# The end of the first phase of a long-convolution kernel: the last rows of the first two pairs are copied straight from result tiles, and the stores and the filter's work there are placed anew

## The chip, the cores and the metric

The kernel runs on one core of a Trainium2 chip. The metric is the time of one execution on the device in microseconds (us); the median of the runs is compared. Engines are named as in the profile: PE (TensorE), DVE (VectorE), ACT (ScalarE), POOL (GpSimd) and SP (SyncE, which here only issues DMAs). A DMA can be issued by SP, ACT or POOL; each of the three has its own queue, and the profile shows an issue by SP or ACT as an instruction of SPq or ACTq.

## The reference

```python
def _attn_ref(x, v, pos_emb, w1, w2):            # x, v: (4, 12800, 128)
    h_filt = (np.maximum(pos_emb @ w1, 0.0) @ w2) * np.exp(-0.01 * pos)[:, None]
    u = x * v
    Uf = np.fft.rfft(u, n=2 * S, axis=1)         # S = 12800
    Hf = np.fft.rfft(h_filt, n=2 * S, axis=0)
    y = np.fft.irfft(Uf * Hf[None], n=2 * S, axis=1)[:, :S]
    return x * y
...
def _moe_ref(x, w_val, conv_w, w_out):           # x is what _attn_ref returned
    gate = sigmoid(causal convolution of x over 5 steps, by channel)
    return (gate * (x @ w_val)) @ w_out
```

So the kernel multiplies x by v, convolves the product along the sequence with a filter as long as the sequence, multiplies by x again and passes the result through a small gated layer.

## The kernel before, in words

The sequence of 12800 is cut into two halves of 6400 (index j), and each half into 100 x 64 (indices n1 and n2). A transform over n1 and one over n2 take the place of the long transform. The kernel has three phases that follow one another, because each needs what the one before left in memory (the HBM).

**First phase** (`signal`, lines 357 to 406, and `filt`, 225 to 297). For each of the 64 values of n2, SP loads 100 rows of x and v (line 312), DVE multiplies them and forms sums and differences (`prep`: lines 323, 334, 335, 342), PE transforms over n1 (line 391, two halves c = 0 and 1 of four records each), ACT copies each half from PSUM into a result tile `st` (line 392), and the tile is stored to `a_u` in HBM (line 400). The tile has 2 x 1024 numbers on each of 100 partitions: the partition is the frequency k of the transform over n1, spread over the 128 partitions by the table `PARTS` (64 frequencies on the even partitions, 32 and 4 between them). The store is three DMAs: frequencies 0 to 63 by ACT, 64 to 95 by POOL, and 96 to 99 by POOL one n2 later (`flush`, line 415). For the last two n2 (62 and 63) the first of them is cut again: frequencies 0 to 3 by SP, 4 to 63 by ACT. An even n2 fills rows n2 and n2 + 1 of `a_u`, an odd one rows 63 + n2 and 64 + n2; so n2 62 fills rows 62 and 63, and n2 63 rows 126 and 127.

Between these, the filter's own transform is advanced step by step. A list `due` (lines 419 to 422) has three spans with a number of steps each; a step is run when the loop has reached its n2. The third span has 26 steps from n2 38.5 on, spread over 22 n2. One step of it has 8 matmuls of PE (16 records, line 292), four scaled copies and one PSUM copy of ACT (lines 279 and 295) and one product of DVE (line 280). The order on every engine is the order in which the program is written (`manual_schedule`).

**Second phase** (from line 462, its loop from 552). It goes over 50 pairs p of frequencies. Pair p takes frequencies 2p and 2p + 1 of all 128 rows of `a_u` (1 MB, `load_a`, line 201) and filter values (`filter_pair`); PE transforms over n2 into `z_ps` (`spectrum`, line 491, 8 records), DVE multiplies by the filter in four instructions (va, vb, vc, vd, line 497), POOL adds (lines 578 and 581), PE transforms back, and the results are stored. `spectrum` of a pair needs all of its 128 rows.

At the border the loads of pair 0 are cut into EARLY rows (0 to 55 and 64 to 119), loaded when n2 = 58 is reached, and LATE rows (56 to 63 and 120 to 127), loaded when the first phase is written out. Pair 1 is loaded behind them, with pairs 2 and 3 after it. On PE, `filter_pair(0)` and ten matmuls whose results nobody reads (lines 561 to 564) come between the last n2 and the first `spectrum`.

**Third phase** (from line 613). Rows of the result are loaded, transformed and gated; PE bounds it.

The loads of x and v go through a ring of nine tiles; a tile is loaded again when the n2 that read it are done (`release`, `fetch`). Two of the last results use tiles of that ring (`SPARE`): n2 61 one of the extra tiles, n2 63 the tile that pair 2 is loaded into afterwards.

Of the kernel before, what the change touches and what calls it, by code (L numbers as in the profile page):

```python
# [23 lines left out]
B, S, D, FO, KC = 4, 12800, 128, 64, 5  # L24
# [93 lines left out]
def tile_longconv_gate(  # L118
# [20 lines left out]
    nc = tc.nc  # L139
# [45 lines left out]
    BD = B * D  # L185
    NP = N1 // 2
    PG = KG // 2
    EARLY, LATE = (slice(0, 56), slice(64, 120)), (slice(56, 64), slice(120, 128))
    weights, loaded = {}, {}

    def load_w(p):
# [17 lines left out]
    with tc.tile_pool(name="p1", bufs=1) as p1, tc.tile_pool(name="ps1", bufs=1, space=PSUM) as ps1:  # L209
# [147 lines left out]
        def signal():  # L357
            fetch(4)
            load_pos(0)
            fetch()  # L360
            load_pos(HC)
            ready = [prep(0)]
            for n in range(N2):
                if n == 8:
                    nc.gpsimd.dma_start(out=dft, in_=t_dft)
                    nc.gpsimd.dma_start(out=tw, in_=t_tw)
                    nc.gpsimd.dma_start(out=inv, in_=t_inv)
                if n == 12:
                    for dst, src in ((wval, w_val), (wout, w_out), (cw, conv_w.rearrange("k d -> d k"))):
                        raw = p1.tile(list(dst.shape), mybir.dt.int64, name=f"raw{len(raws)}")  # L370
                        nc.gpsimd.dma_start(out=raw, in_=src)
                        raws.append((dst, raw))
                if n in (18, 22, 26):
                    _narrow(nc, p1, *raws[n // 4 - 4])
                if n == BACK + 2:
                    load_w(0)
                if n == N2 - 6:
                    for part in EARLY:
                        load_a(0, part)
                if n + 1 < N2:  # L380
                    ready.append(prep(n + 1))
                both = ready.pop(0)
                if n in SPARE:
                    st = next(t for i, t in ring if i == SPARE[n]).rearrange("p (c e) -> p c e", c=2)
                else:
                    st = p1.tile([128, 2, J * BD], F32, name="st", bufs=4)
                for c in range(2):
                    fp = ps1.tile([128, J, BD], F32, name="fp", bufs=2)
                    for j in range(J):
                        h = slice(j * 64, j * 64 + 64)  # L390
                        nc.tensor.matmul(out=fp[:, j], lhsT=fsd[h, c], rhs=both[c][h], start=True, stop=True)  # L391
                    nc.scalar.copy(out=st[:, c], in_=fp.rearrange("k j e -> k (j e)"))  # L392
                    yield
                src = st.rearrange("k c e -> k (c e)")
                row = n % 2 * N2 + n // 2 * 2
                dst = a_u[:, row:row + 2].rearrange("k c e -> k (c e)")
                for eng, (k0, k, step, p0) in zip((nc.scalar, nc.gpsimd), PARTS):
                    cuts = [0, 4, k] if k0 == 0 and n >= N2 - 2 else [0, k]
                    for a, b in zip(cuts, cuts[1:]):
                        (nc.sync if b == 4 else eng).dma_start(  # L400
                            out=dst[k0 + a:k0 + b], in_=src[p0 + step * a:p0 + step * (b - 1) + 1:step])
                if n % 2 == 1:
                    release()
                rest.append((dst, src))
                if len(rest) > 1 or n + 1 == N2:
                    flush()
# [10 lines left out]
        n_done = [False]  # L417

        due, t0 = [], 3
        for n, w in ((J * N2 // 4 + 2, 15.5), (FO // 2, 20), (N1 // 4 + 1, 22)):  # L420
            due += [t0 + w * i / n for i in range(n)]
            t0 += w
        sig, fil = signal(), filt()
# [38 lines left out]
    with tc.tile_pool(name="p2", bufs=1, reuse_waits="tile") as p2, \  # L462
# [89 lines left out]
        with tc.manual_schedule():  # L552
            for p in range(-1, NP + 2):
                now, nxt, old = 0 <= p < NP, p + 1 < NP, 0 <= p - 1 < NP
                if p < 0:
                    z_first = new_z()
                    for part in LATE:
                        load_a(0, part)
                    for part in EARLY + LATE:
                        load_a(1, part)  # L560
                    filt_p[0] = filter_pair(0)
                    for _ in range(10):
                        w_ps = ps2.tile([128, 2, BD], F32, name="c_ps", bufs=2)
                        nc.tensor.matmul(
                            out=w_ps[:, 0, 0:2 * D], lhsT=ident, rhs=dft.rearrange("p a k -> p (a k)"), start=True, stop=True)
                if (p + 3) % PG == 0 and p + 3 < NP:
                    load_w(p + 3)
                for q in range(2, AHEAD) if p < 0 else (p + AHEAD,):
                    if q < NP:
                        load_a(q, slice(0, 2 * N2))  # L570
                if now:
                    h = filt_p.pop(p)
                    z0, z1 = z_p.pop((p, 0)), z_p.pop((p, 1))
                    va = p2.tile([128, 2 * J, B, D], F32, name="va", bufs=3)
                    vb = p2.tile([128, 2 * J, B, D], F32, name="vb", bufs=2)
                    times(va, z0[:, 0], h[:, 0], 2 * J)
                    times(vb, z0[:, 1], h[:, 1], 2 * J)
                    (nc.gpsimd if nxt else nc.vector).tensor_tensor(va[:, 0:2], va[:, 0:2], vb[:, 0:2], op=ALU.add)  # L578
                    apart = p % 6 == 5
                    if not apart:  # L580
                        nc.gpsimd.tensor_tensor(va[:, 2:4], va[:, 2:4], vb[:, 2:4], op=ALU.add)  # L581
                if nxt:
                    z_p[p + 1, 0] = spectrum(p + 1, 0, z_first if p < 0 else None)
                if now:
                    vc = p2.tile([128, 2, B, D], F32, name="vc", bufs=2)
                    vd = p2.tile([128, 2, B, D], F32, name="vd", bufs=2)
                    times(vc, z1[:, 0], h[:, 0, 0:2], 2)
                    times(vd, z1[:, 1], h[:, 1, 0:2], 2)
                    v_p[p] = [va[:, 2:4]] + [vb[:, 2:4]] * apart + [vc, vd]
                if now and not nxt:  # L590
                    inverse(p, va[:, 0:2])
                if old:
                    inverse_half(p - 1, v_p.pop(p - 1))
                if p + 2 < NP:
                    filt_p[p + 2] = filter_pair(p + 2)
                if nxt:
                    z_p[p + 1, 1] = spectrum(p + 1, 1)
                if now and nxt:
                    inverse(p, va[:, 0:2])
                if 0 <= p - 2:  # L600
                    butterfly(p - 2)
                for s, c, i in early.get(p, ()):
                    load_part(s, c, i)
# [277 lines left out]
```

## Time and profile before

| | |
|---|---|
| median of 3 runs | 1068.43 us (1066.77 to 1068.98) |
| the profiled execution's own time | 1070.6 us |
| its span in the profile | 1068.8 us |
| mean granted clock of TensorE | 0.977 |
| busy share of the span | PE 92%, DVE 91%, ACT 58%, POOL 70% |
| DMA traffic | 330.16 MB, mean 309 GB/s |

Times in the trace count from the span's start; the profiled execution's own time is 1.8 us more than its span. The numbers in brackets behind an engine's row are the idle time ahead of the instruction and what ended it. The first phase ends near 314 us, the second near 676 us.

### The profile page before, as it was taken

To read this page: it belongs to the slowest core of one execution; us is meant where nothing else is said; L and a number is where in the kernel's file an instruction comes from. 1 tells how busy PE (TensorE), PEld (TensorE's weight loads), DVE (VectorE), ACT (ScalarE), POOL (GpSimd) and SP (SyncE) were. 2 spreads that over 40 slices of the span, in tenths; PEclk is the share of its full clock that TensorE was granted. 3 is DMA by queue.
4 is the path that set the end of the run, shared out by engine and by line. 5 is a ranking of instruction groups with operands and counts; after the bars stand their busy time and mean duration, and the time that the engine had idled before them with its cause. 6 is when DMAs were issued, how large, how long until landed. Compare 5 with 4: busy or idle time off the path is not lost. (4 is left out here: it accounts for less than half of the span.)

```text
span 1068.8 us, 21559 instructions
## 1 busy us (share of the span) xinstructions
PE 980.4 (92%) x8100; PEld 510.5 (48%) x8100; DVE 972.3 (91%) x1061; ACT 624.9 (58%) x1017; POOL 747.6 (70%) x465
## 2 busy tenths in 40 slices
PE   2768799989998999999999999679999999999996
PEld 0344466656644555455445545334444444444442
DVE  8868999599948999999989999279999999999997
ACT  1545477788862444444434444267677777777774
POOL 2223222222225999999999999689999999999990
PEclk9889899999998999999999999899999999999999
DMA  8999899998989899989989988977788888888813
GB/s 276 372 347 378 329 370 374 384 344 326 388 279 309 317 330 332 334 313 337 344 309 331 345 319 272 342 293 264 273 293 312 270 296 300 278 300 285 298 70 123
DMA packets 97151, 330.16 MB, mean 309 GB/s; under 512 B 12690, under 2 KB 37882, under 8 KB 81050
## 3 DMA queue, kind: packets, MB, share of 16 engines
q1 hardware_dynamic: 41864, 196.96, 54.4%
q10 hardware_dynamic: 49506, 111.30, 26.8%
q0 software_dynamic: 5680, 20.53, 5.0%
q8 instruction: 66, 1.08, 0.4%
q14 instruction: 35, 0.29, 0.1%
HBM read 197.67 MB, written 131.07 MB: 308 GB/s over the span
## 5 line engine op out<-in xcount | busy, mean ns | idle before, releaser
L696 POOL TENSOR_TENSOR ext<-yr,xr 128x400 f32<-128x400 f32 x120 | 308.3, 2570 | 27.3 <-DVE yr L694 24.0
L713 DVE SCALAR_TENSOR_TENSOR gt<-ext,cw,gt 128x1600 f32<-128x1600 f32 (+1 forms) x132 | 240.8, 1824 | 0.1
L400 POOL DMA_DIRECT2D a_u<-st x62 | 33.2, 536 | 225.8 <-ACT st L392 222.0
L392 ACT COPY st<-fp 128x1024 f32<-128x1024 f32 x124 | 125.9, 1030 | 85.4 <-PE fp L391 46.4
L542 POOL TENSOR_TENSOR c_both<-c_raw 128x512 f32<-128x512 f32 x100 | 126.5, 1295 | 9.2 <-DMA c_z<-c_both 6.2
L671 PE MATMUL sd<-ld,inv 128*64 128x512 f32 x512 | 126.4, 612 | 7.2 <-DMA ld<-c_y 6.9
L497 DVE TENSOR_TENSOR va<-z_ps,h_sb 128x2048 f32<-128x2048 f32 x50 | 114.0, 2280 | 18.3 <-PE z_ps L491 18.2
L578 POOL TENSOR_TENSOR va<-va,vb 128x1024 f32<-128x1024 f32 x49 | 117.1, 2390 | 19.0 <-DVE vb L497 18.9
L535 ACT COPY c_raw<-c_ps 128x1024 f32<-128x1024 f32 x50 | 50.8, 1015 | 134.5 <-PE c_ps L530 118.1
L497 DVE TENSOR_TENSOR vb<-z_ps,h_sb 128x2048 f32<-128x2048 f32 x50 | 114.2, 2283 | 11.6 <-POOL va L581 11.6
L676 ACT COPY sd_sb<-sd 128x512 f32<-128x512 f32 x128 | 75.9, 593 | 74.0 <-PE sd L671 62.1
L491 PE MATMUL z_ps<-ld,ld 64*64 64x512 f32 x800 | 111.1, 612 | 8.7 <-DVE vb L497 4.9
L735 PE MATMUL o_ps<-gd,wout 128*128 128x400 f32 x256 | 111.4, 517 | 8.3 <-DVE gd L730 6.8
L391 PE MATMUL fp<-ld,fsd 64*128 64x512 f32 x320 | 90.4, 670 | 28.5 <-DVE ld L342 14.8
L725 PE MATMUL v_ps<-ext,wval 128*128 128x400 f32 x252 | 105.3, 500 | 0.0
L581 POOL TENSOR_TENSOR va<-va,vb 128x1024 f32<-128x1024 f32 x42 | 101.2, 2409 | 0.0
L507 PE MATMUL c_ps<-va,ld 64*64 64x512 f32 x800 | 97.7, 601 | 3.3 <-DVE va L578 1.4
L683 PEld LDWEIGHTS tp<-ident,sd_sb 128*128 128x128 f32 x512 | 58.6, 141 | 77.0 <-PE sd L671 49.6
L513 ACT COPY c_sb<-c_ps 128x1024 f32<-128x1024 f32 x49 | 49.7, 1013 | 58.5 <-PE c_ps L507 58.5
L683 PE MATMUL tp<-ident,sd_sb 128*128 128x128 f32 x512 | 80.3, 280 | 3.8 <-DVE yr L694 2.7
L735 PEld LDWEIGHTS o_ps<-gd,wout 128*128 128x128 f32 x256 | 42.7, 189 | 58.5 <-ACT sd_sb L676 15.4
L730 DVE TENSOR_TENSOR gd<-v_ps,sg 128x400 f32<-128x400 f32 x126 | 70.1, 556 | 0.2 <-ACT sg L718 0.2
(116 smaller groups left out, 1808.8 us busy)
## 6 DMA issues: line engine op xcount, KB each, us to landing
ld<-a_u SPq DMA_DIRECT2D x48, 1024.0 KB
a_u<-st ACTq DMA_DIRECT2D x61, 512.0 KB
xr<-in_xt_dram SPq DMA_DIRECT2D x32, 800.0 KB
c_y<-c_sb ACTq DMA_DIRECT2D x49, 512.0 KB
out_dram<-o_sb ACTq DMA_DIRECT2D x31, 800.0 KB
c_z<-c_both ACTq DMA_DIRECT2D x48, 512.0 KB
ld<-in_xv_dram SPq DMA_DIRECT2D x40, 512.0 KB
ld<-c_y SPq DMA_DIRECT2D x32, 512.0 KB
```

What stands on the lines that cost most here:

```text
L392: nc.scalar.copy(out=st[:, c], in_=fp.rearrange("k j e -> k (j e)"))
L491: nc.tensor.matmul(out=z[half[h], c], lhsT=wk[half[c], 0, half[h]], rhs=a2[half[c], h, j], start=True, stop=True)
L497: nc.vector.tensor_tensor(out, z.rearrange("p (b d) -> p b d", d=D).unsqueeze(1).to_broadcast([128, n, B, D]), h_sb.unsqueeze(2).to_broadc ...
L542: nc.gpsimd.tensor_tensor(both[:, :, m], raw[:, :, 1], raw[:, :, 0], op=op)
L578: (nc.gpsimd if nxt else nc.vector).tensor_tensor(va[:, 0:2], va[:, 0:2], vb[:, 0:2], op=ALU.add)
L581: nc.gpsimd.tensor_tensor(va[:, 2:4], va[:, 2:4], vb[:, 2:4], op=ALU.add)
L671: nc.tensor.matmul(out=to, lhsT=inv[:, 2 if j * m * c else c], rhs=t, start=True, stop=True)
L683: nc.tensor.transpose(out=tp[:, b], in_=t[:, b], identity=ident)
L696: nc.gpsimd.tensor_tensor(e[:, r0 + r], yr, xr, op=ALU.mult)
L713: nc.vector.scalar_tensor_tensor(gt, rows(t, k)[:, cols], cw[:, k:k + 1], gt, op0=ALU.mult, op1=ALU.add)
L725: nc.tensor.matmul(out=v_ps, lhsT=wval, rhs=rows(t)[:, r * ROW:(r + 1) * ROW], start=True, stop=True)
L735: nc.tensor.matmul(out=o_ps, lhsT=wout, rhs=gd, start=True, stop=True)
```

## The change

1. Pairs 0 and 1 no longer get their rows of n2 62 and 63 by way of `a_u`. Eight small DMAs copy them from the result tile into the pair's tile: for each of the two n2, each of the two pairs and each of its two frequencies, one partition of `st` (8 KB) goes to two partitions of the pair's tile. For n2 62 SP issues all four, for n2 63 ACT issues the two of pair 0 and SP the two of pair 1.
2. LATE shrinks from 8 to 6 rows in each half. LATE of pair 0 is written ahead of the copies of n2 62, LATE of pair 1 behind them. EARLY of pair 1 is loaded at n2 60. All were written at the start of the second phase, or, for EARLY of pair 0, at n2 58, where it stays.
3. The stores of frequencies 0 to 63: for n2 60 and 61 SP takes them from ACT, in two DMAs (0 to 3, 4 to 63). For n2 62 and 63 POOL stores 4 to 63; 0 to 3 are not stored at all for these rows, since nobody loads them any more.
4. The 26 steps of the filter's third span are spread over 20 n2, so the last runs at n2 58.0 where it ran at 60.0.

```diff
-    EARLY, LATE = (slice(0, 56), slice(64, 120)), (slice(56, 64), slice(120, 128))
+    EARLY, LATE = (slice(0, 56), slice(64, 120)), (slice(56, 62), slice(120, 126))
...
-                if n == N2 - 6:
+                if n in (N2 - 6, N2 - 4):
                     for part in EARLY:
-                        load_a(0, part)
+                        load_a((n - N2 + 6) // 2, part)
...
+                row = n % 2 * N2 + n // 2 * 2
                 src = st.rearrange("k c e -> k (c e)")
-                row = n % 2 * N2 + n // 2 * 2
                 dst = a_u[:, row:row + 2].rearrange("k c e -> k (c e)")
-                for eng, (k0, k, step, p0) in zip((nc.scalar, nc.gpsimd), PARTS):
-                    cuts = [0, 4, k] if k0 == 0 and n >= N2 - 2 else [0, k]
+                last = n >= N2 - 2
+                if n == N2 - 2:
+                    for part in LATE:
+                        load_a(0, part)
+                for q in range(2 * last):
+                    for k in range(2):
+                        p0 = 2 * (2 * q + k)
+                        (nc.scalar if n == N2 - 1 and q == 0 else nc.sync).dma_start(
+                            out=loaded[q][row:row + 2, k].rearrange("c j e -> c (j e)"), in_=st[p0:p0 + 1])
+                if n == N2 - 2:
+                    for part in LATE:
+                        load_a(1, part)
+                ends = (nc.gpsimd, nc.gpsimd) if last else (nc.sync, nc.gpsimd) if n >= N2 - 4 else (nc.scalar, nc.gpsimd)
+                for eng, (k0, k, step, p0) in zip(ends, PARTS):
+                    cuts = [0, k] if k0 or n < N2 - 4 else [4, k] if last else [0, 4, k]
                     for a, b in zip(cuts, cuts[1:]):
-                        (nc.sync if b == 4 else eng).dma_start(
-                            out=dst[k0 + a:k0 + b], in_=src[p0 + step * a:p0 + step * (b - 1) + 1:step])
+                        eng.dma_start(out=dst[k0 + a:k0 + b], in_=src[p0 + step * a:p0 + step * (b - 1) + 1:step])
...
-        for n, w in ((J * N2 // 4 + 2, 15.5), (FO // 2, 20), (N1 // 4 + 1, 22)):
+        for n, w in ((J * N2 // 4 + 2, 15.5), (FO // 2, 20), (N1 // 4 + 1, 20)):
...
                 if p < 0:
                     z_first = new_z()
-                    for part in LATE:
-                        load_a(0, part)
-                    for part in EARLY + LATE:
-                        load_a(1, part)
                     filt_p[0] = filter_pair(0)
```

## The prediction, on record before the run

> **What bounds the kernel now.** I began with what DVE waits for after the first phase, because DVE is nearly full in the second. The rows below give the idle time, how often, and the longest; then stand the four products of a pair.
>
> ```profile
> DVE va L497 <- PE z_ps L491: 18.2, 2, 17.9
> DVE vb L497 <- POOL va L581: 11.6, 15, 1.9
> ...
> L497 DVE TENSOR_TENSOR vb<-z_ps,h_sb 128x2048 f32<-128x2048 f32 x50 | 114.2, 2283 | 11.6 <-POOL va L581 11.6
> L497 DVE TENSOR_TENSOR va<-z_ps,h_sb 128x2048 f32<-128x2048 f32 x50 | 114.0, 2280 | 18.3 <-PE z_ps L491 18.2
> ```
>
> Beside one wait of 17.9 us, DVE idles 11.6 us in 50 pairs, and POOL, which sets those idles, works on what DVE hands it. So the whole second phase hangs on the instant at which DVE starts the first va, and the third phase hangs on the second: a microsecond there is a microsecond at the end. The timeline by engine around that wait (start, duration, idle before in brackets):
>
> ```profile
> 304.52 2.50 DVE L342 TENSOR_TENSOR ld<-ld 128x512 f32<-128x512 f32 x4
> 324.95 2.29 DVE L497 TENSOR_TENSOR va<-z_ps,h_sb 128x2048 f32<-128x2048 f32 x1 [17.93 <-PE z_ps L491]
> 338.49 2.28 DVE L497 TENSOR_TENSOR va<-z_ps,h_sb 128x2048 f32<-128x2048 f32 x1
> ...
> 308.60 0.46 ACTq L400 DMA_DIRECT2D a_u<-xv  x1
> 309.24 1.93 ACT L392 COPY st<-fp 128x1024 f32<-128x1024 f32 x2 [0.66 <-PE fp L391]
> 311.19 0.92 ACTq L400 DMA_DIRECT2D a_u<-st  x1
> 312.29 1.93 ACT L392 COPY ld<-fp 128x1024 f32<-128x1024 f32 x2 [1.12 <-PE fp L391]
> 314.24 0.83 ACTq L400 DMA_DIRECT2D a_u<-ld  x1
> 315.17 0.59 ACT L478 COPY h_sb<-c_ps 128x512 f32<-128x512 f32 x1 [0.96 <-PE c_ps L564]
> ...
> 301.81 2.05 PE L292 MATMUL gp<-g_sb,ag 128*128 128x128 f32 x16
> 303.80 1.99 PE L391 MATMUL fp<-xv,fsd 64*128 64x512 f32 x8
> 307.71 2.04 PE L391 MATMUL fp<-ld,fsd 64*128 64x512 f32 x8 [0.55 <-ACT xv L392]
> 316.36 2.86 PE L564 MATMUL c_ps<-dft,ident 128*128 128x256 f32 x12 [0.52 <-ACT h_sb L480]
> 319.14 1.08 PE L491 MATMUL z_ps<-ld,ld 64*64 64x512 f32 x4
> 323.50 0.65 PE L491 MATMUL z_ps<-ld,ld 64*64 64x512 f32 x2 [3.28 <-DMA ld<-a_u]
> 336.41 1.09 PE L491 MATMUL z_ps<-ld,ld 64*64 64x512 f32 x8 [0.29 <-PE c_ps L507]
> ...
> 311.19 0.65 SPq L400 DMA_DIRECT2D a_u<-st  x1
> 313.49 0.27 SPq L201 DMA_DIRECT2D ld<-a_u  x1
> 314.24 0.62 SPq L400 DMA_DIRECT2D a_u<-ld  x1
> 319.47 5.12 SPq L201 DMA_DIRECT2D ld<-a_u  x8
> 323.17 1.41 SPq L201 DMA_DIRECT2D ld<-a_u  x3
> ```
>
> The chain: the last copy of a result ends at T = 312.29 + 1.93 = 314.22. SP stores its first four frequencies at 314.24 and can issue the last LATE load of pair 0 only when that store has landed, at 319.47, 5.23 us later (for n2 62 the same took 313.49 - 311.19 = 2.30). Meanwhile PE has run the unread matmuls and half of the first `spectrum` (319.14, four records) and stops; it resumes at 323.50, and DVE starts at 324.95. From T to DVE that is **10.73 us**.
>
> **The change part by part. First, the way through memory.** For pairs 0 and 1 the store, its landing and the load behind it go; one copy takes their place. What is next on the path? On ACT the copies of n2 63 are followed by two DMA issues for pair 0. The trace has no issue of such a shape; the nearest are 0.27 (64 KB load) and 0.65 (32 KB store), so two take 0.54 to 1.30. Before, one issue of 0.83 stood there and L478 began 0.95 behind T. So the filter copies start at -0.3 to +0.4 against before, and the unread matmuls, which wait for them (316.36), end between T + 4.6 and T + 5.3 (before 319.14 - T = 4.92). The first `spectrum` is then whole, 8 records in 1.09 (row of 336.41), and DVE follows 0.1 later: T + 5.8 to T + 6.5. I take **T + 6.3**, beyond the middle, since the new issues resemble a store of few partitions.
>
> That holds if the copies land by T + 4.9. The later of ACT's two is issued near T + 0.46 to T + 0.65. By the two landings above it is there at T + 2.8 to T + 5.9; in the latter case DVE starts 1.45 behind it (323.50 to 324.95), at T + 7.3. I take the first as decisive: ACT's queue has held nothing since n2 59, while the 5.23 fell to a store on SP whose queue still had a load to do. The matmuls cover 2 us beyond it.
>
> The Trainium skill speaks against this: "DMA: Bandwidth & Descriptors", section "Queues, rings and completion order", says that a DMA's completion mark is ordered behind every earlier write of the same DMA engine, across its queues. By that rule the copies would not be known as done before POOL's bulk store of n2 62 on those engines is, and the sum would use 5.23 in place of 2.30. Both rows above agree with it in kind: one store, 2.30 and 5.23.
>
> **The moved loads and SP's order.** Behind n2 61's stores SP has: LATE of pair 0 (waits for the landing of n2 61), four copies of n2 62, LATE of pair 1, two copies of n2 63. With the results 2.2 us apart (below) n2 61 is done at T - 4.4; landing at the worst 5.23 puts SP at T + 0.9, four issues of 0.65 at T + 3.5; pair 0's two copies, issued by T + 2.2, land 2.30 later, at T + 4.5, still in time. EARLY of pair 1 is now next in SP's order behind EARLY of pair 0 (first row below), so it moves from 319.47 to about 294.4, ahead of the stretches of the other rows:
>
> ```profile
> 292.99 1.38 SPq L201 DMA_DIRECT2D ld<-a_u  x2
> ...
> 300.00:305.00 5.00, 5.00 (x30) 3.13 (x32) 4.93 (x5) 3.91 (x9) 1.11 (x2) 1.00 0.90 330
> 305.00:310.00 5.00, 3.96 (x16) 0.90 (x12) 2.02 (x4) 3.68 (x4) 1.64 (x3) 1.00 0.63 249
> 310.00:315.00 5.00, 4.58 (x30) 1.92 (x30) 0.00 (x0) 3.09 (x4) 2.19 (x4) 1.00 0.74 243
> ```
>
> (The last two columns are DMA's busy share and GB/s.) Its 0.9 MB need 2.8 us at 330 GB/s and push other transfers back by so much; 305 to 315 leaves room of 0.37 x 5 + 0.26 x 5 = 3.1 for them. Without that cover stores would land up to 2.8 us later, which the slack of SP just worked out would no longer hold: then DVE starts some 2 us later.
>
> **POOL's stores.** POOL gets two stores of 480 KB, one more issue for each n2:
>
> ```profile
> 313.02 0.53 POOL L400 DMA_DIRECT2D a_u<-st  x1
> 315.62 0.58 POOL L415 DMA_DIRECT2D a_u<-ld  x1
> 329.59 2.35 POOL L578 TENSOR_TENSOR va<-va,vb 128x1024 f32<-128x1024 f32 x1 [13.40 <-DVE vb L497]
> ...
> DMA to landing us min/median/max: 3.0/5.2/7.4
> ...
> q0 software_dynamic: 180, 0.62, 43.8%
> ...
> DMA packets 212, 0.74 MB, mean 185 GB/s; under 512 B 31, under 2 KB 31, under 8 KB 212
> ```
>
> (The fourth row is the time from POOL's issues to their landing, the fifth POOL's queue from 314 to 319.4 us, the last all DMA from 324 to 328.) Four issues after T' (I write T' for T in the changed kernel) at 0.53 to 0.58 end near T' + 2.2; POOL's first add (329.59) comes 4.6 us behind DVE's first va, so they are hidden. The last lands 7.4 later, T' + 9.1, and load 2 of the three at 323.17, pair 2, can go (before: T + 8.95). DVE needs pair 2 338.49 - 324.95 = 13.54 behind its start, at T' + 19.8. Even at 185 GB/s 1 MB takes 5.7: hidden, with 5 us to spare.
>
> **The filter's span and ACT's queue.** They set T'. ACT's cycle in the tail is 1.93 of copies and 0.66 idle, in which it issues a store. With SP and POOL storing, the limit becomes one half's matmuls behind the other half's copy: about 1.0 + 1.0 + 0.2 = 2.2 us per n2 instead of 2.59. The last copies also lose the 1.12 - 0.66 = 0.46 behind the longer issue at 311.19. From PE's n2 62 (307.71) to T it takes 6.51; without these 0.46 and 0.4, 5.65.
>
> *Early bound.* DVE has n2 62's operands half way through 304.52 + 2.50, at 305.8. If the filter's steps are out of PE's way, n2 62 starts then: T' = 305.8 + 5.65 = **311.4**. DVE's own work isn't changed in sum.
>
> *Late bound.* PE's list isn't shorter. These rows show how much idle time it has to absorb the steps that move ahead:
>
> ```profile
> 252.00:284.00 32.00, 29.53 (x186) 19.58 (x186) 29.94 (x38) 26.97 (x56) 7.79 (x14) 1.00 1.01 396
> 285.00:305.00 20.00, 20.00 (x125) 13.09 (x125) 19.80 (x23) 16.73 (x33) 4.89 (x9) 1.00 0.94 352
> ...
> PE gp L292 <- ACT ag L295: 4.1, 6, 1.1
> ```
>
> PE is full from 285 to 305. If nothing is absorbed, the last step (end 303.86) ends only the two n2 earlier that now follow it, 2 x 1.99: 299.9. Then 5.5 n2 remain where 3.5 did: 10.36 (314.22 - 303.86) + 2 x 2.59 - 0.46 - 3 x 0.4 gives T' = **313.8**. Two steps close on one another make PE wait for ACT (4.1 us in 6 waits); the denser list has four more such places, which at 0.7 each make 316.6. Of PE's 2.5 us idle in 252 to 284 I let a third be used: T' = **313.0**, nearest to the bound without new waits; -1.2.
>
> **Sum.** DVE starts at 313.0 + 6.3 = 319.3 instead of 324.95: -5.65. The profiled execution would take 1070.6 - 5.65 = 1064.95 (its span of 1068.8, and 1.8 around it); it stood 2.2 above the median, so the median goes from 1068.43 to **1062.8**.
>
> **The rivals.**
> *The copies land late* (20%): like the store of 314.24, with bulk stores on the same engines. DVE at T' + 7.3 = 320.3: -4.65, 1063.8. For it: the 5.23; against: an empty queue of ACT. The Trainium skill's rule above, in "DMA: Bandwidth & Descriptors", would make this the case.
> *The denser filter costs the tail* (12%): T' = 316.6, DVE at 322.9: -2.05, 1066.4. For it: PE's full rows and the waits for ACT; against: DVE's unchanged sum.
> *Pair 0 still waits for the stores to memory* (5%), whatever is copied, if what the loads and matmuls wait for includes them: DVE 1.45 behind T' + 9.1, at 323.5: -1.4, 1067.0.
> *Slower* (6%): POOL's queue becomes the bound of pair 2. In 314 to 319.4 that queue moved 0.62 MB, 115 GB/s; from n2 62 on it has 1.6 MB, by that rate until about T' + 13, and pair 2 would be loaded at T' + 18.7, just in time for T' + 19.8. It decides from some T' + 14 on, and eats the gain at T' + 20. At half the rate it ends near T' + 27 and DVE stands 13 us: 1068.43 - 5.65 + 13 = 1075.8. Against it: before, supply and not the queue's rate held those 0.62 MB back, since they were issued one by one from 313.02 to 315.62.
>
> **How the numbers follow.** The forecast has 57%: its own range is T' 311.4 with + 5.8 (317.2, -7.75: 1060.7) to T' 313.8 with + 6.5 (320.3, -4.65: 1063.8). The range for 8 in 10 goes on over the late copies to the denser filter, 1066.5, and at the low end to 1060.4 for the scatter of the runs. Faster by over 0.2% (2.1 us, about what a measurement of this kernel can tell from no change): forecast, late copies and half of the dense filter, 0.83; within: the other half and pair 0's wait, 0.11; slower: 0.06.
>
> **What would show it.** Right: `spectrum` of pair 0 follows the unread matmuls without idle time on PE; DVE's wait ahead of the first va is 10 to 13 us; no DVE wait ahead of pair 2's va. T' itself, the last result copy's end, tells the filter's part. Wrong: PE idle between the matmuls and z_ps with a DMA as its end (late copies); PE waits of L292 for ACT grown by over 2 us (dense filter); a DVE wait for z_ps near 13 us behind the first va (POOL's queue).

## The result and the profile after

The changed kernel is slower. Its median is 1081.95 us (1080.94 to 1083.5, three runs) against 1068.43 (1066.77 to 1068.98): 1.0115 times the time before, with a 95% interval of 1.0093 to 1.0137. The forecast was 1062.8, with a range of 1060.4 to 1066.5. The profiled execution took 1081.95 us, its span is 1080.2, which is 11.4 more than the span before.

The waits of DVE in the second phase, and DVE's timeline around them (start, duration, idle time before in brackets), say at once where it went:

```profile
DVE va L509 <- PE z_ps L503: 22.8, 1, 22.8
DVE vb L509 <- POOL va L589: 11.4, 15, 2.2
```

```profile
307.53 1.23 DVE L323 TENSOR_TENSOR ld<-ld 128x1024 f32<-128x1024 f32 x1 [2.96 <-PE fp L391]
...
311.19 2.50 DVE L342 TENSOR_TENSOR ld<-ld 128x512 f32<-128x512 f32 x4
336.47 2.29 DVE L509 TENSOR_TENSOR va<-z_ps,h_sb 128x2048 f32<-128x2048 f32 x1 [22.79 <-PE z_ps L503]
```

The first va starts at 336.47, where it started at 324.95: 11.52 later. From there to the end it is 1080.2 - 336.47 = 743.7 us, before 1068.8 - 324.95 = 743.9. So here the second and third phase passed the delay on one to one, as the prediction had it, and all of the loss lies at the border. (That the two times agree within 0.2 us is partly luck: over all 19 profiles of this document it is 739.7 to 748.3 us from the first va to the end, with no trend in whether the first va is early or late.) It has two parts. The timelines of ACT, PE and SP of the changed kernel:

```profile
314.20 1.93 ACT L392 COPY st<-fp 128x1024 f32<-128x1024 f32 x2 [2.15 <-DMA a_u<-st]
316.45 1.93 ACT L392 COPY ld<-fp 128x1024 f32<-128x1024 f32 x2 [0.31 <-PE fp L391]
326.16 2.01 ACTq L404 DMA_DIRECT2D ld<-ld  x2
328.21 0.59 ACT L490 COPY h_sb<-c_ps 128x512 f32<-128x512 f32 x1 [9.84 <-DMA ld<-st]
```

```profile
317.84 2.97 PE L572 MATMUL c_ps<-dft,ident 128*128 128x256 f32 x8
329.40 5.49 PE L572 MATMUL c_ps<-dft,ident 128*128 128x256 f32 x12 [8.60 <-ACT h_sb L492]
334.82 1.42 PE L503 MATMUL z_ps<-ld,ld 64*64 64x512 f32 x8
```

```profile
301.71 3.86 SPq L201 DMA_DIRECT2D ld<-a_u  x4
309.80 1.57 SPq L413 DMA_DIRECT2D a_u<-st  x2
312.08 1.71 SPq L413 DMA_DIRECT2D a_u<-xv  x2
319.64 2.45 SPq L201 DMA_DIRECT2D ld<-a_u  x2
322.14 3.50 SPq L404 DMA_DIRECT2D ld<-st  x4
325.68 0.76 SPq L201 DMA_DIRECT2D ld<-a_u  x2
327.36 1.22 SPq L404 DMA_DIRECT2D ld<-ld  x2
```

**The end of the last result copy, T', is 316.45 + 1.93 = 318.37** (the trace's own end of it), 4.15 later than before, where 1.2 earlier was forecast. **From T' to the first va it is 18.10 us**, where it was 10.73 and 6.3 was forecast: 7.37 more. 4.15 + 7.37 are the 11.52.

In the second part ACT is the engine to read. Its two small copies for pair 0, forecast for 0.5 us behind T', are issued from 326.16 on, 7.8 behind it. Its filter copies (L490) stand behind them in ACT's order and start at 328.21; the last twelve unread matmuls wait for those (8.60 us idle), and spectrum follows them. ACT waits there for a DMA that it did not issue: `ld<-st` is a copy of n2 62, issued by SP. The same time in stretches of 5 us (length of the stretch, busy time of PE, PEld, DVE, ACT and POOL, granted clock, DMA's busy share, GB/s):

```profile
305.00:310.00 5.00, 3.91 (x18) 1.08 (x16) 2.43 (x3) 3.86 (x4) 2.11 (x4) 1.00 1.01 290
310.00:315.00 5.00, 2.94 (x14) 0.90 (x12) 3.65 (x6) 2.72 (x3) 1.65 (x3) 1.00 0.98 382
...
320.00:325.00 5.00, 0.75 (x3) 0.30 (x2) 0.00 (x0) 0.00 (x0) 0.90 (x2) 1.00 0.97 349
325.00:330.00 5.00, 0.59 (x2) 0.51 (x3) 0.00 (x0) 1.14 (x3) 0.00 (x0) 0.53 0.24 79
330.00:335.00 5.00, 5.00 (x16) 3.55 (x18) 0.00 (x0) 0.00 (x0) 0.00 (x0) 0.50 0.68 242
335.00:340.00 5.00, 2.54 (x32) 0.85 (x32) 3.53 (x2) 1.14 (x3) 0.00 (x0) 0.95 1.03 409
```

The room of 3.1 us in the DMA engines between 305 and 315 is gone: the busy share is 1.01 and 0.98, where it was 0.63 and 0.74. From 320 to 325 hardly any engine works (PE 0.75 us, POOL 0.90) while the DMA engines are full. And after PE's 8.6 us of idle time its clock is at half: the twelve matmuls take 5.49 us, before 2.86. That alone is 2.6 of the 7.37. The Trainium skill has this in "TensorE: Matmul & The Clock Gate", section "Part 1: The HAM clock gate": after an idle window of some 3.4 us the array runs at half rate, and at full rate again after a busy window of that length. The granted clock of 0.50 agrees. By the last three rows the clock was at half for some 10.2 us, of which the last 6.1 came after PE had resumed at 329.40, so the way back took longer here than one such window.

For the first part the waits of the first phase are the view. First DVE's from 207 to 318.4 us and SP's from 207 to 300 in the kernel before, then the same two in the changed kernel:

```profile
DVE ld L323 <- issue: 1.9, 1, 1.9
```

```profile
SPq L312 <- PE fp L391: 32.1, 10, 8.6
```

```profile
DVE ld L323 <- DMA ld<-in_xv_dram: 3.7, 1, 3.7
DVE ld L323 <- PE fp L391: 3.0, 1, 3.0
DVE xv L323 <- DMA xv<-in_xv_dram: 2.1, 1, 2.1
```

```profile
SPq L312 <- PE fp L391: 42.7, 10, 11.7
```

SP waits 10.6 us longer for PE's matmuls before it may load the next x and v into a tile of the ring, and DVE, which waited 1.9 us for its operands, waits 8.8. (The row of 3.0 names PE; the trace's record of that instruction's waits ends with the landing of a load, at 307.34, and in a second profile of this kernel, e9, the row of the same instruction names the load, 3.84.) The EARLY loads that stand behind the last load in SP's order move from 292.99 to 301.71.

### The profile page after: what moved, and what is told of

Its sections match the earlier page's. It is cut to its first block, busy times and chain, and to the rows that moved or that the text cites. A ratio compares the mean times of both kernels' runs of the same rounds, so it can differ in the third digit from the quotient of the medians.

```text
span 1080.2 us, 21562 instructions
## 1 busy us (share of the span) xinstructions
PE 981.2 (91%) x8100; PEld 511.8 (47%) x8100; DVE 972.4 (90%) x1061; ACT 625.4 (58%) x1017; POOL 748.7 (69%) x467
## 5 line engine op out<-in xcount | busy, mean ns | idle before, releaser
L509 DVE TENSOR_TENSOR vb<-z_ps,h_sb 128x2048 f32<-128x2048 f32 x50 | 114.2, 2284 | 11.4 <-POOL va L589 11.4
L503 PE MATMUL z_ps<-ld,ld 64*64 64x512 f32 x800 | 107.7, 604 | 8.7 <-DVE vb L509 4.2
```

The lines of the kernel that those rows point to most:

```text
L503: nc.tensor.matmul(out=z[half[h], c], lhsT=wk[half[c], 0, half[h]], rhs=a2[half[c], h, j], start=True, stop=True)
L509: nc.vector.tensor_tensor(out, z.rearrange("p (b d) -> p b d", d=D).unsqueeze(1).to_broadcast([128, n, B, D]), h_sb.unsqueeze(2).to_broadc ...
```

## The experiments

T' and the distance from T' to the first va were read in every profile. The ratio is to the kernel before, run beside it on the same chip; "pair 1" says when its EARLY rows are loaded, "copies" who issues the four copies for pair 0.

| run | kernel | T' | first va behind T' | ratio (95%) |
|---|---|---|---|---|
| | before: span 22, pair 1 at the border, no copies | 314.2 | 10.7 | 1 |
| | changed: span 20, pair 1 at n2 60, copies by SP and ACT | 318.4 | 18.1 | 1.0115 (1.0093 to 1.0137) |
| e9 | the changed kernel again | 318.3 | 16.6 | 1.0074 (1.0046 to 1.0102) |
| e1 | changed, span 22 | 311.5 | 16.8 | 1.0003 (0.9983 to 1.0023) |
| e2 | before, span 20 | 320.1 | 10.9 | 1.0042 (1.0016 to 1.0069) |
| e3 | changed, all copies by SP | 317.4 | 13.6 | 1.0059 (1.0037 to 1.008) |
| e4 | changed, pair 1 at the border | 321.7 | 8.9 | 1.0051 (1.0024 to 1.0077) |
| e5, e15 | span 22, pair 1 at the border | 312.9, 312.1 | 8.6, 7.6 | 0.9984 (0.9961 to 1.0008), 1.0 (0.9981 to 1.002) |
| e6 | span 22, pair 1's copies and LATE last | 310.6 | 13.1 | 0.9993 (0.9966 to 1.0019) |
| e7 | e5 and e6 together | 317.7 | 6.9 | 0.9993 (0.9973 to 1.0013) |
| e8 | before, only the stores changed | 311.0 | 15.5 | 0.999 (0.9969 to 1.0011) |
| e10 | span 22, EARLY of pair 1 by ACT at n2 58 | 314.4 | 13.4 | 1.0014 (0.9991 to 1.0037) |
| e11 | e7 with span 24 | 312.8 | 7.4 | 1.001 (0.9987 to 1.0033) |
| e12 | e7 with five unread matmuls | 317.7 | 9.8 | 1.0002 (0.9978 to 1.0026) |
| e13 | changed, copies by POOL | 318.8 | 8.3 | 1.0033 (1.0007 to 1.006) |
| e14, e17 | span 22, pair 1 at the border, copies by POOL | 312.4, 316.1 | 7.2, 7.2 | 0.9977 (0.9956 to 0.9999), 0.9972 (0.9954 to 0.999) |
| e16 | span 22, pair 1 at n2 60, copies by POOL | 309.7 | 8.6 | 0.9979 (0.9957 to 1.0) |

A single T' says little: with one and the same span of 22 it lies between 309.7 and 317.7. But the twelve profiles with 22 have a mean of 313.4, and the six with 20 one of 319.1 (317.4 to 321.7), 5.7 later.

**The filter's span.** e1 is the changed kernel with the old span, e2 the old kernel with the new one:

```diff
-        for n, w in ((J * N2 // 4 + 2, 15.5), (FO // 2, 20), (N1 // 4 + 1, 20)):
+        for n, w in ((J * N2 // 4 + 2, 15.5), (FO // 2, 20), (N1 // 4 + 1, 22)):
```

> The changed kernel with the filter's third span back at 22 n2. Theory (late releases): the denser filter makes PE late, so x and v of n2 63 are loaded 8.6 us later (299.7 against 291.1), DVE waits, and the EARLY loads that stand behind that load on SP collide with the last stores. With 22 the load of n2 63 is issued near 291, T' (end of the last result copy) is 312.5 to 314 instead of 318.4, SP issues LATE of pair 0 by T' or earlier, and T' to the first va shrinks from 18.1 to 8 to 11 us: first va at 321 to 325, 1065 to 1069 us. Rival (the wait of ACT's copies belongs to the new queue order, whatever the filter): T' to the first va stays 16 to 18 us, first va near 331, 1074 us.

> The kernel before with the filter's third span at 20 n2 and nothing else. Theory (late releases): T' goes from 314.2 to 317.5 to 318.5, with DVE waits for loads of 6 to 9 us in place of 1.9, and T' to the first va stays 10.7 us: 3.5 to 4.5 us slower, 1072 to 1073 us. Rival (T' is late because EARLY of pair 1 and SP's stores load the DMA engines, not by the filter): T' within 1 us of 314.2, 1068 us.

Of e2, first DVE's waits from 207 to 318.4 us and SP's from 207 to 302, and then a row of DVE's timeline and one of ACT's:

```profile
DVE ld L323 <- DMA ld<-in_xv_dram: 6.5, 2, 3.6
```

```profile
SPq L312 <- PE fp L391: 42.4, 10, 10.0
```

```profile
307.45 1.23 DVE L323 TENSOR_TENSOR ld<-ld 128x1024 f32<-128x1024 f32 x1 [3.60 <-DMA ld<-in_xv_dram]
```

```profile
318.16 1.93 ACT L392 COPY ld<-fp 128x1024 f32<-128x1024 f32 x2 [1.11 <-PE fp L391]
```

With nothing but the span changed, SP's wait for PE (42.4) and DVE's waits for loads come as in the changed kernel, T' is 320.1, the first va still 10.9 behind it, and the time 0.42% longer. In e1 it is the other way round: SP waits 29.0 us for PE, T' is 311.5, and the time is that of before. So the span makes T' late, by itself and without the other edits. It does not make the distance: that stays at 16.8 in e1, as the rival of that run had it and not its theory (8 to 11). By n2 57 the 26 steps at a pace of 20 have put (57 - 38.5) x (26/20 - 26/22) = 2.2 more steps ahead of it in PE's list, 2.2 x 2.0 = 4.4 us as PE is full; its operands' tiles come free later, SP loads the last n2 into them later, and DVE waits. That load goes out 8.6 us later (299.67, before 291.09), so the 4.4 are about half of it; what makes the other half, no run separates. PE's list is shorter afterwards, but there PE lacks operands: in the changed kernel it is busy for 2.94 of the 5 us from 310 to 315, where it was for 4.58.

e9 is the changed kernel a second time, beside other variants:

> The changed kernel itself, beside variants on the same chip. The theory (the shorter span makes the tail of the first phase stall, and the copies are known as landed late because of what stands ahead of them): 1.009 to 1.013 of the time before, the last result copy T' at 317 to 320 us, the first va 16 to 18.5 us behind it. The rival, that the loss belongs to one odd profile: ratio below 1.006.

T' and the distance are as in the first profile; the ratio, 1.0074, is below what was expected, with the whole interval still above 1. e11 goes on to a span of 24, on top of the two edits of e7:

> The kernel of the run e7 (EARLY of pair 1 at the border, pair 1's copies and LATE behind pair 0's) with 24 n2 for the filter's third span in place of 22. If a longer span makes the releases of the ring still earlier: T' 310 to 313, the first va 7 us behind it, 0.996 to 0.998 of the time before. The rival: the last steps of the filter now stand between the last n2 on PE, T' 1 to 3 us later than with 22, ratio 0.999 to 1.002.

T' 312.8 is no earlier than the mean with 22, and the time is not told from before: from 22 on, the span isn't what bounds.

**Who holds the copies.** ACT waited for a copy of SP's. In the program as built, each DMA of SP or ACT reports its landing on one of eight counts that go round in turn over both queues, and it isn't issued before the DMA that used the same count, the one eight earlier in the order of the program, has landed. For ACT's first copy that is the first LATE load of pair 0, for its second the first copy of n2 62. The semaphore records of the changed kernel's trace show the same: the first LATE load, issued at 319.64, has landed at 326.06, and ACT's first copy goes out at 326.16; the first copy of n2 62, issued at 322.14, has landed at 327.52, and ACT's second goes out at 327.55. With EARLY of pair 1 moved ahead, LATE of pair 0 and these copies themselves stand behind it. SP's waits from 295 to 345 in the changed kernel tell what LATE waited for:

```profile
SPq L201 <- DMA ld<-a_u: 3.1, 1, 3.1
SPq L201 <- DMA a_u<-st: 2.7, 1, 2.7
SPq L201 <- DMA a_u<-xv: 1.9, 1, 1.9
```

The first wait is for EARLY of pair 1 (the same count again), the second for n2 60's first four frequencies, stored at 309.80 and landed only at 319.62, the third, ahead of the second LATE load, for those of n2 61, stored at 312.08 and landed at 321.78. So two things come together: with the DMA engines full, small transfers of SP take 5.4 to 9.8 us to land, and the rotation hands this on to ACT. Four edits test parts of it. e3 gives ACT's two copies to SP, e4 loads EARLY of pair 1 at the border again:

```diff
-                        (nc.scalar if n == N2 - 1 and q == 0 else nc.sync).dma_start(
+                        nc.sync.dma_start(
```

```diff
-                if n in (N2 - 6, N2 - 4):
+                if n == N2 - 6:
                     for part in EARLY:
-                        load_a((n - N2 + 6) // 2, part)
+                        load_a(0, part)
...
                     z_first = new_z()
+                    for part in EARLY:
+                        load_a(1, part)
```

> The changed kernel with all eight copies of partitions issued by SP, none by ACT. Theory (ACT's filter copies stand behind its two copy issues, which wait for LATE of pair 0): ACT starts the filter copies 0.3 us behind T' (near 318.7, not 328.2), PE's unread matmuls are over by T' + 5, and the first va waits for SP's last copies alone, issued near 326 to 328: first va near 331, 5 us less than the changed kernel, 1076 to 1078 us. Rival (the copies' landing itself is late, because the DMA engines are full): the first va stays near 336, 1081 us.

> The changed kernel with EARLY of pair 1 loaded at the start of the second phase again (behind the copies of n2 63), its tile chosen at n2 60 as in the changed kernel. Theory (0.9 MB of EARLY of pair 1 stand ahead of n2 60's and 61's stores in SP's queue): LATE of pair 0 is issued 2 to 4 us earlier than 319.6, T' stays near 318, first va at 331 to 334, 1076 to 1079 us. Rival (the filter alone makes LATE late): within 1 us of the changed kernel, 1081 to 1083 us.

PE in e3, then DVE and ACT in e4:

```profile
316.83 5.56 PE L572 MATMUL c_ps<-dft,ident 128*128 128x256 f32 x20
326.58 3.44 PE L503 MATMUL z_ps<-ld,ld 64*64 64x512 f32 x6 [4.19 <-DMA ld<-st]
```

```profile
309.86 1.23 DVE L326 TENSOR_TENSOR ld<-ld 128x1024 f32<-128x1024 f32 x1 [7.96 <-DMA ld<-in_xv_dram]
```

```profile
321.81 2.53 ACTq L409 DMA_DIRECT2D ld<-ld  x2
324.38 0.59 ACT L495 COPY h_sb<-c_ps 128x512 f32<-128x512 f32 x1 [2.65 <-PE c_ps L579]
```

In e3 ACT is free, the unread matmuls run without a break and end at 322.4; then PE waits 4.19 us for a copy of n2 62, which SP could issue only from 320.37 on. The distance falls to 13.6 (changed kernel: 16.6 and 18.1) and no further. In e4 ACT's copies go out at 321.81, just behind T' (321.7), and the distance is 8.9. T' itself is the latest of all, behind a wait for a load of 7.96 us: EARLY of pair 1 isn't what delays T'. e5, e6 and e7 repeat the question with the span at 22. e6 and e7 write pair 1's copies and its LATE load behind pair 0's:

```diff
-                if n == N2 - 2:
-                    for part in LATE:
-                        load_a(1, part)
...
+            for s, at in ends62:          # behind the loop over n2
+                copies(1, s, at, nc.sync)
+            for part in LATE:
+                load_a(1, part)
```

> The changed kernel with the span at 22 n2 and EARLY of pair 1 loaded at the start of the second phase. Theory (with EARLY of pair 1 out of the way the small copies land soon, so what ACT waits for ends soon): T' 311 to 313 as with 22 alone, ACT issues its second copy by T' + 1 instead of T' + 8.1 (319.59), first va at T' + 8.9 as in the run with EARLY of pair 1 at the border and 20 n2: 320 to 322, 3 to 5 us faster than the kernel before, about 1066 us beside 1069.8. Rival (the 16.8 us belong to the new queue order alone): first va 327 to 329, as the kernel before or slower.

> The changed kernel with the span at 22 n2, and the four copies and the LATE loads of pair 1 written behind all of pair 0's. By the rotation of completion counts, ACT's two copies then wait for n2 61's small store and for the second LATE load of pair 0, not for SP's first copy (which took from 312.1 to 319.6 with 22 alone); the traffic is the same. Theory (ACT's filter copies are late because of what ACT's copies wait for): ACT's second copy by 316, filter copies start by 317, first va at 322 to 324, 2 to 3 us faster than before. Rival (the traffic itself is late, not the waits): first va 327 to 329, no difference to 22 alone (1071).

> The two edits of the two runs above together (span 22, EARLY of pair 1 at the border, pair 1's copies and LATE behind pair 0's). If the waits and the traffic both count: T' 311 to 313, ACT's copies by T' + 1, first va at T' + 6.5 to 8, 318 to 320.5: 4.5 to 6 us faster than before, 1064 to 1065. If only one of them counts, no better than the better of the two.

ACT in e6:

```profile
311.46 4.51 ACTq L420 DMA_DIRECT2D ld<-ld  x2
316.07 0.59 ACT L495 COPY h_sb<-c_ps 128x512 f32<-128x512 f32 x1 [5.44 <-DMA ld<-a_u]
```

The load at the border brings the distance to 8.6, the order alone to 13.1, both together to 6.9. e6 is the test of the rotation itself: the filter copies start at 316.07 (forecast by 317), where they started at 320.32 with 22 alone, and the wait ahead of them now ends with a LATE load, not with a copy of SP's, as the rotation said. By the semaphore records ACT's first copy waited there for n2 61's small store to `a_u`, issued at 306.18 and landed at 311.36, which has nothing to do with the tile that the copy writes, so a dependency by tile is not the reason. The times fell short of what these three runs were expected to show (2 to 6 us faster): none is told from before, and T' was 317.7 in e7, not 311 to 313. e10 keeps the early load but has ACT issue it:

```diff
                 if n == N2 - 6:
                     for part in EARLY:
                         load_a(0, part)
+                    for part in EARLY:
+                        load_a(1, part, nc.scalar)
```

> Span 22, and the EARLY rows of pair 1 are issued by ACT when n2 58 is reached, ahead of n2 60, not by SP behind the load of n2 63: the same traffic before the border, out of SP's queue and some us sooner. If the late hand-over (16.8 us with span 22) came from SP's order, the first va stands 9 to 11 us behind T' and the time is 0.997 to 1.000 of before. If it comes from the traffic itself and from the LATE load behind it, 14 to 17 us and 1.000 to 1.003.

13.4 lies between the two: SP's order isn't the whole, and neither is the traffic. In the eleven profiles in which ACT issues pair 0's two copies, ACT's first filter copy starts 1.6 to 9.8 us behind T', and the first va follows 5.3 to 8.3 us behind that start: the distance is ACT's delay and a rest that changes far less. e8 puts only the new stores into the kernel before:

> The kernel before with the stores of the change alone: n2 60 and 61 by SP in two parts, of n2 62 and 63 frequencies 4 to 63 by POOL and 0 to 3 by SP; no copies, EARLY and LATE as before, span 22. Theory (ACT's issues cost the tail 0.4 us per n2 and 0.46 at the end, which gave 22 alone its T' of 311.5): T' 311.5 to 312.5, T' to first va 10 to 11 us, 1.5 to 2.5 us faster, 1068. Rival (the loads' timing gave that T', not the stores): T' 314.

The time doesn't change (0.999). In its profile T' is early (311.0) and the distance long, 15.5 where 10 to 11 was expected: pair 0's LATE loads wait for the small stores of n2 62 and 63, which SP issues as before but which now land later (issued at 308.82 and 314.14, the loads behind them at 313.75 and 321.89). e12 takes half of the unread matmuls from e7 (`for _ in range(5)`):

> The kernel of the run e7 with five instead of ten unread matmuls ahead of the first spectrum (what is computed is the same, since nobody reads them). If the hand-over is now bounded by PE's list behind the filter copies: the first va 5 to 6 us behind T' (6.93 in e7). The rival: the copies' landing bounds it, 6.5 to 8 us behind T', PE idle ahead of z_ps with a DMA as its end. Time 0.996 to 1.000 of before by the one, 0.998 to 1.001 by the other.

PE then waits for a copy (1.55 us, `ld<-ld`) and the distance is 9.8, not shorter than in e7 and longer than the rival had it: the ten matmuls are a cover for the landing.

**The copies on a queue with counts of its own.** POOL's DMAs report on eight other counts. e13 is the changed kernel with one edit:

```diff
-                        (nc.scalar if n == N2 - 1 and q == 0 else nc.sync).dma_start(
+                        (nc.sync if q else nc.gpsimd).dma_start(
```

> The changed kernel (span 20, EARLY of pair 1 at n2 60) with pair 0's four copies issued by POOL, ahead of its stores. If the hand-over is late because the copies wait in the rotation of SP and ACT, ACT's first filter copy starts within 1 us of T', the unread matmuls end 5 us behind T', and the first va waits only for the LATE load: 8 to 10.5 us behind T', 1.002 to 1.006 of the time before. If small transfers land late in the traffic whatever the queue: 12 us or more behind T', PE idle ahead of z_ps with a DMA as its end, 1.006 to 1.010. T' itself stays at 316 to 320 us by both.

ACT, PE and DVE in e13:

```profile
316.83 1.93 ACT L392 COPY ld<-fp 128x1024 f32<-128x1024 f32 x2 [0.31 <-PE fp L391]
318.66 0.59 ACT L490 COPY h_sb<-c_ps 128x512 f32<-128x512 f32 x1
```

```profile
318.23 6.54 PE L572 MATMUL c_ps<-dft,ident 128*128 128x256 f32 x20
324.70 1.79 PE L503 MATMUL z_ps<-ld,ld 64*64 64x512 f32 x6
```

```profile
327.02 2.29 DVE L509 TENSOR_TENSOR va<-z_ps,h_sb 128x2048 f32<-128x2048 f32 x1 [12.70 <-PE z_ps L503]
```

The same eight copies beside the same loads and stores, with EARLY of pair 1 still at n2 60 and T' still at 318.8: the filter copies follow the last result copy without a gap, PE doesn't stop, and the distance is 8.3 in place of 16.6 to 18.1. POOL's four copies take 4.4 to 4.7 us from issue to landing. Small transfers that land late on any queue would have shown 12 or more. So some 8 to 10 us of the distance were the rotation, and ACT's and PE's work that stood behind it. That it is the counts, and no other property of POOL's queue or of its order, rests on the waits in the built program and the trace, and on e6; no run changed the counts alone. The time moves less than the distance: 1.0033, against 1.0074 and 1.0115. e16 takes the span back as well, e14 and e17 also load EARLY of pair 1 at the border:

> The changed kernel with two edits: span 22, and pair 0's copies issued by POOL; EARLY of pair 1 stays at n2 60. If the rotation was the whole of what the early load cost, T' is 311 to 314 us, the first va 6.5 to 8.5 us behind it, and the time 0.996 to 0.999 of before. If the load's traffic costs by itself, the LATE load and the copies land later: 9 to 12 us behind T', 0.998 to 1.002.

> The kernel of e5 (span 22, EARLY of pair 1 at the border) with pair 0's four copies issued by POOL. By the rotation theory the first va comes 6 to 7.5 us behind T' (8.55 in e5), and the time is 0.995 to 0.999 of before; by the traffic theory 8 to 10 us behind T' and 0.998 to 1.001. T' scatters between 311 and 318 us.

> The kernel of e14 again: first va 6.5 to 8 us behind T', 0.996 to 0.9995 of the time before. If e14's 0.9977 was scatter: 0.9995 to 1.002.

> The kernel of e5 again: first va 7 to 9.5 us behind T', 0.996 to 1.000 of the time before. If the 0.9984 of e5 was scatter: 0.999 to 1.002.

PE and DVE in e16:

```profile
309.19 6.53 PE L572 MATMUL c_ps<-dft,ident 128*128 128x256 f32 x20
315.65 2.14 PE L503 MATMUL z_ps<-ld,ld 64*64 64x512 f32 x6
```

```profile
318.33 2.29 DVE L509 TENSOR_TENSOR va<-z_ps,h_sb 128x2048 f32<-128x2048 f32 x1 [14.95 <-PE z_ps L503]
```

The distance is 8.6 with the early load and 7.2 without it (twice), so on POOL's queue the early load may cost some 1.4 us by itself; between two profiles of one kernel the distance differed by up to 1.5 (18.1 and 16.6), so this is a hint only. The kernel of e14 and e17 is faster than before by 0.2 to 0.3%, if barely: e17's interval ends at 0.999, e14's at 0.9999. e16, 0.9979, ends at 1.0 and isn't quite told from before; e15, the border of e14 with the copies on SP and ACT, is not told from before either, nor, by their intervals, from e14. Thus the change can be worth something once the copies land soon and the span stays; how much of it is the way around memory, no run separates from the moved stores (e8, stores alone: 0.999). The profile of e17 has the first va at 323.35, 1.6 us earlier than before, e16 at 318.33, 6.6 earlier, with T' at the late and the early end of its spread.

## Why the prediction was wrong, step by step

**"DVE's own work isn't changed in sum", and T' = 313.0** failed: 318.37, and a mean of 319.1 over the six profiles with a span of 20. The step looked for the cost of moved filter steps in PE's idle time and in PE's waits for ACT, and took DVE's operands to come as before. Their sum is unchanged, but DVE waits 8.8 us for them, since loads wait for PE to release the ring's tiles. The late bound, 313.8, had PE's earlier n2 end 2 x 1.99 later and missed what hangs on just that. The rival of the denser filter gave 316.6 by another path, PE's waits of L292 for ACT, which did not grow (3.6 us, before 4.1). One more wait, of ACT for a store to leave a result tile (2.15 ahead of 314.20), was not in the sum either; e9 has it not, and T' is the same there.

**"The later of ACT's two is issued near T + 0.46 to T + 0.65"** failed by 7 us and more: 326.16 and, 1.4 later, the second. "ACT's queue has held nothing since n2 59" was true of what ACT issued and said nothing of what its DMAs wait for. The step then fell on everything behind it: filter copies, unread matmuls, PE's clock.

**EARLY of pair 1, "from 319.47 to about 294.4", hidden in a room of 3.1 us**: it was issued between 304.33 and 305.57 at the end of SP's row of 301.71, because SP was late for the first reason, right where n2 60's to 62's stores want the same DMA engines. The price named for lost cover, 2 us, was too low: in e4 the distance falls to 8.9, 7.7 to 9.2 less. With the copies on POOL the early load costs about 1.4 (e16 against e14 and e17, within what one kernel scatters); the rest came through the rotation.

**SP's order**: "landing at the worst 5.23 puts SP at T + 0.9, four issues of 0.65 at T + 3.5". The landing was mis-sized: n2 60's and n2 61's small stores took 9.8 and 9.7 us. LATE's first issue at 319.64 is T' + 1.3, which nearly fits; the second, which waits for n2 61's store, came at 321.83, T' + 3.5, although n2 61 was done at T' - 6.3 and not at T - 4.4. The four copies then took 3.50, and so these are done at 325.64, T' + 7.3.

**T' + 6.3 itself** is near the mark where nothing holds the copies: 7.2 in e14 and e17. In e14 PE's unread matmuls end 5.9 behind T', not 4.6 to 5.3, and DVE follows 1.3 behind the start of spectrum (forecast 1.2). So the term is 0.9 too small; why the matmuls end later is not shown. "I take the first as decisive", a landing of 2.30, can't be read from the changed kernel's own copies on ACT, as their issue was late. But the copy of n2 62 on SP took 5.4 us to land, and of POOL's copies those of n2 63 took 4.1 to 4.7 in e13, e14, e16 and e17: nearer to 5.23, so the term was too small, and the unread matmuls covered it. e7 and e14 have no wait of PE for a copy, e12, with less cover, has one of 1.55. Whether the completion order across queues that the prediction quoted from the Trainium skill has a share in those landings was not separated by any run.

**What held**: phases two and three pass a delay on one to one (over the 19 profiles the span grows by 0.95 us for 1 us of the first va, with some us of scatter); POOL's stores are hidden (its last issue ends at 320.9, T' + 2.5, forecast T' + 2.2) and pair 2 has no wait, since the wait of va in the second phase is one wait; the last two result copies follow at 316.45 - 314.20 = 2.25 us where 2.2 was worked out. The rival on the slower side, POOL's queue, is therefore wrong; the loss had two other mechanisms, which no rival named.

**What stays open**: why T' lies between 309.7 and 317.7 with one span. It goes with the instant at which SP issues the load of n2 63: in seven profiles with a span of 22 that is 287.9 to 289.4, and T' 309.7 to 312.9; in the other five it is 290.4 to 293.4, and T' 314.2 to 317.7 (with 20: 298.2 to 299.9 and 317.4 to 321.7). What moves that load from run to run was not tried. The second phase, from the first va to DVE's last product in it, also differs between profiles, 344.8 to 352.2 us. So the end of one profile says less than the distance at the border, and a first va that is some us earlier is only in part seen in the medians: e16's profile has it 10.0 us earlier than e1's, its median ratio is only 0.0024 lower, 2.6 us.

## What to carry to other kernels

Work moved ahead in a full engine's list delays what stands behind it, and the tiles that this releases: ask which loads wait for those releases before you count the work as shifted at no cost. Before you put a small DMA on an idle queue, look up what the built program makes it wait for; if completion counts are shared in rotation, it can stand behind a load or a copy of another queue that lands late, and so does all that its engine does next. A queue with counts of its own took 8 us off the distance here, of which the time of the whole kernel showed 0.4 to 0.8%.

## What the runs showed that was not expected

- DMAs of SP and ACT hold one another up through eight shared completion counts: the same copies stood 7.8 us behind T' on ACT, and ran without holding anybody on POOL (distance 16.6 to 18.1 against 8.3).
- PE's clock: after 8.60 us of idle time the granted clock was 0.50 to 0.53 over 10 us, and matmuls that took 2.86 took 5.49. The length of one wait does not tell by itself: two records of spectrum took 1.12 to 1.22 in e3, after 4.19 us idle, and 1.12 in e2, after 2.90, but 0.65 in the kernel before, after 3.28.
- With the DMA engines full, the small store of n2 60 took 9.8 us to land (309.80 to 319.62) and that of n2 61 9.7 (312.08 to 321.78), where before the change n2 62's took 2.30 and n2 63's 5.23.
- One program's first phase ends at different times in two profiles: 312.4 in e14, 316.1 in e17.
